# A state-space kernel on one core: the table that orders its 821 operations is written anew

## Chip, cores and metric

The kernel runs on one core of one Trainium2 chip. Times are device microseconds (us) of that core; less is better. The engines are called as the profile calls them: PE (matrix engine; PEld is its weight load), DVE (vector), ACT (scalar), POOL (GpSimd) and SP, which here only issues transfers.

## What is computed

Two sequence operators stand side by side; sequence length is 2048, width 640, everything in bf16. The left half is a diagonal complex state-space layer, the right half a gated long convolution.

```python
# left: A
Lam_bar = exp(exp(log_dt) * (Lambda_re + 1j * Lambda_im))
Bu = einsum("bld,pd->blp", x, ((Lam_bar - 1) / Lam)[:, None] * B)
h[t] = Lam_bar * h[t - 1] + Bu[t]                    # 2048 steps
a = 2 * real(einsum("blp,dp->bld", h, C)) + x * Dskip
# right: B
kv = (sum over t < 4 of shifted(k, t) * shift_k[:, t]) * v
b = q * (causal_convolution(kv, ssm_k) + kv * ssm_D)
out = concatenate([a, b], axis=-1)
```

## The kernel before, in words

Every operation is added to a list by `Program.add` with a name and a number (its place in the list). Most are one instruction; an operation on PE is a group of matmuls into one or two PSUM banks, and its eviction (a copy of the banks to SBUF by ACT or DVE) is an operation of its own. `ORDER` (line 1136) is a string with one entry for each operation: number, engine (A for ACT, V for DVE, G for POOL, T for PE, S for SP) and first bank; a small `t` says that PE does the operation in halves of 64 columns. `Program.emit` (line 123) walks the table and issues each operation on its engine, with waits on those that write or read the same memory or hold the same bank. So the order on each engine is the order of the table, each engine works strictly in that order, and nothing is decided at run time. SP issues nearly all transfers, ACT three at the start.

The left half (`PartA`). `load_B` (line 516) fetches B: blocks 0 and 1 by plain transfers (L524), turned on PE (L531) and evicted by ACT (L533); the rest by two transposing transfers (L519, "the rest of B"). `load_x` (L554) fetches x in eight transposing transfers. `warm` (L546) gives PE ten pairs of matmuls on zeros while it would be idle. `params` (from L357) loads Lambda and log_dt (L369), transposes them by one matmul (L377, "the parameter matmul") and computes powers of Lam_bar on DVE, ACT and POOL, in part by sines (L415, L420, L463). Then the scan in a tree: `up2`, `up1`, `up0` (L588 and L609, evictions L605, L629, L655), a coarse scan on DVE (`coarse`, L673 to L697, with its matmuls at L226 and L230), and `down` (L226, L230, evictions L733, L735). `project` multiplies 16 sets of 128 rows by C (20 matmuls at L226, or 40 at L230), adds x times Dskip (L744) and stores the rows (L780); C comes by L563 and is scaled by L578, evicted at L582. Evictions of `project` are at L768 (ACT, then added at L776) or L770 (DVE).

The right half (`PartB`), in two halves of 320 channels. `load_kv` (L833) fetches k and v of 128 channels by one transposing transfer each, five times (0 to 4); `conv` makes the four taps (L206 or L207, sums L859, product with v L860); `plane` writes the product to DRAM (L866), `relay` reads it back in another layout (L876). `load_h` fetches the filter (L826), a small ssm_D (L813) is added to it at L828. The convolution is a Fourier transform by matmuls: `s1` (L895, in quarters L900; evicted L905), `s2` (L919; L932), a product on DVE or POOL (L943 to L950), back by `r2` (L970; L975) and `r1` (L991; L1007 or L1009, and L1014), times q (L844), stored at L1025.

Some memory is used twice. The half of `VT` that takes the first v is before that scratch for tables: `f1` (DVE, L291) and `i_s` (ACT, L326) read it, and the transfer of the first v waits for both. The groups of `r2` of one half need the whole product of that half (they read what L943 to L950 write).

## Time and profile before

| | |
|---|---|
| median of three runs | 189.14 us (187.04, 189.92, 189.14) |
| the profiled execution | 187.05 us |
| its span, first to last instruction | 185.2 us (1.85 us lie around it) |
| busy PE / PEld / DVE / ACT / POOL | 175.5 / 123.7 / 157.1 / 146.7 / 72.6 us |
| first `up2` group starts, last matmul ends | 9.28 us, 181.8 us |
| granted PE clock | 1.00 |

"L588 PE MATMUL acc<-arena" is a matmul of line 588 that reads the arena (all SBUF memory of the kernel is one tile, `arena`, and all PSUM one, `acc`). In square brackets a row of the timeline gives the idle time before it and what ended it. In the table by stretches each engine has its busy time and the number of its instructions.

### The profile page before, as it was taken

The page shows a single profiled execution, that of the slowest core. Times are in us where ns is not written, and L with a number is a line of the kernel's source. Part 1 is how long each engine was busy: PE and PEld are TensorE (multiplying, and loading weights), DVE is VectorE, ACT ScalarE, POOL GpSimd, SP SyncE. Part 2 cuts the span into 40 slices and gives each one's busy share as a digit, 9 for nine tenths or more (in the row PEclk, how much of TensorE's full clock was granted, in tenths as well). Part 3 has the DMA queues.
Part 4 walks back from the last instruction along what each step waited for, and adds up shares of the span by engine and source line. Part 5 has one row for each costly group of instructions (what it writes and reads, how often), then busy time and mean ns, then how long its engine had stood idle before and what let it go on. Part 6 is the DMA issues. An engine that isn't in the chain of part 4 may idle for free.

```text
span 185.2 us, 7657 instructions
## 1 busy us (share of the span) xinstructions
PE 175.5 (95%) x3399; PEld 123.7 (67%) x3399; DVE 157.1 (85%) x227; ACT 146.7 (79%) x181; POOL 72.6 (39%) x69
## 2 busy tenths in 40 slices
PE   7999999999999999887999999999999999999992
PEld 3554666645768766566686588777578876887771
DVE  3538858699759899998988999999999999898971
ACT  2469697999999998998998998997998883985000
POOL 8669999910000000016704925740730000550630
PEclk9999999999999999999999999999999999999999
DMA  5999999899999989899998479402494993058895
GB/s 156 200 176 141 217 156 130 158 184 192 243 229 225 242 146 164 168 159 164 143 164 225 155 152 128 74 4 85 126 198 107 213 234 86 7 173 200 204 226 159
DMA packets 106827, 30.15 MB, mean 163 GB/s; under 512 B 101291, under 2 KB 106155, under 8 KB 106795
## 3 DMA queue, kind: packets, MB, share of 16 engines
q1 hardware_dynamic: 106476, 29.35, 86.6%
q8 instruction: 26, 0.43, 1.1%
q10 hardware_dynamic: 318, 0.33, 0.5%
q14 instruction: 7, 0.05, 0.1%
HBM read 11.32 MB, written 7.86 MB: 104 GB/s over the span
## 4 chain that ended last, share of the span: by engine, by line
PE 46%; ACT 23%; DVE 14%; SPq 7%; issue 5%; DMA 3%; POOL 0%; ACTq 0%; DVEq 0%; POOLq 0%
PE acc L226 16%; ACT arena L905 8%; PE acc L919 8%; PE acc L230 6%; PE acc L588 5%; DVE arena L735 4%; SPq L554 4%; ACT arena L207 3%; PE acc L970 3%; DMA arena<-in_B_k_dram 3%; ACT arena L932 3%; PE acc L609 3%; PE acc L991 3%; SPq L519 3%; ACT arena L355 2%
## 5 line engine op out<-in xcount | busy, mean ns | idle before, releaser
L588 PE MATMUL acc<-arena 128*64 128x512 bf16 x400 | 45.5, 379 | 0.8 <-DVE arena L420 0.7
L932 ACT CAST arena<-acc 128x960 bf16<-128x960 f32 (+1 forms) x43 | 36.3, 925 | 3.3 <-PE acc L919 2.3
L226 PE MATMUL acc<-arena 128*128 128x320 bf16 (+2 forms) x256 | 36.6, 298 | 1.1 <-ACT arena L905 0.7
L905 ACT CAST arena<-acc 128x1024 bf16<-128x1024 f32 x37 | 36.0, 1027 | 2.1 <-PE acc L900 1.9
L588 PEld LDWEIGHTS <-arena 128*64 128x64 bf16 x400 | 24.3, 110 | 18.4 <-DVE arena L420 1.1
L226 PEld LDWEIGHTS <-arena 128*128 128x128 bf16 x256 | 23.7, 98 | 11.2 <-ACT arena L905 0.8
L860 POOL TENSOR_TENSOR arena<-arena 128x2048 bf16<-128x2048 bf16 x2 | 8.8, 4420 | 51.4 <-DVE arena L859 44.6
L919 PE MATMUL acc<-arena 128*64 128x160 bf16 x512 | 23.3, 235 | 0.6 <-ACT arena L905 0.3
L230 PE MATMUL acc<-arena 128*64 128x320 bf16 (+3 forms) x258 | 23.2, 313 | 0.6 <-DVE arena L697 0.6
L919 PEld LDWEIGHTS <-arena 128*64 128x64 bf16 x512 | 18.5, 110 | 7.2 <-ACT arena L932 1.8
L859 DVE TENSOR_TENSOR arena<-arena 128x2048 bf16<-128x2048 bf16 x14 | 17.8, 1268 | 5.0 <-ACT arena L207 4.7
L735 DVE TENSOR_TENSOR arena<-acc,arena 128x1024 bf16<-128x1024 f32 (+2 forms) x19 | 20.4, 1115 | 0.9 <-PE acc L230 0.6
L776 POOL TENSOR_TENSOR arena<-arena 128x640 bf16<-128x640 f32 x3 | 4.2, 1417 | 32.1 <-ACT arena L768 32.1
L975 ACT CAST arena<-acc 128x1024 bf16<-128x1024 f32 x16 | 15.4, 1025 | 1.6 <-PE acc L970 1.5
L230 PEld LDWEIGHTS <-arena 128*64 128x64 bf16 x258 | 13.0, 110 | 3.6 <-issue 0.7
L895 PE MATMUL acc<-arena 128*64 128x128 bf16 x400 | 14.6, 220 | 0.7 <-ACT arena L605 0.3
L895 PEld LDWEIGHTS <-arena 128*64 128x64 bf16 x400 | 12.6, 110 | 3.6 <-ACT arena L905 0.9
L206 DVE TENSOR_SCALAR arena<-arena 128x2048 bf16<-128x2048 bf16 x15 | 11.0, 748 | 3.6 <-DMA arena<-in_B_k_dram 3.4
L770 DVE TENSOR_TENSOR arena<-acc,arena 128x640 bf16<-128x640 f32 (+1 forms) x14 | 10.8, 772 | 3.3 <-PE acc L226 2.5
L207 ACT ACTIVATE arena<-arena 128x2048 bf16<-128x2048 bf16 (+2 forms) x10 | 11.1, 1111 | 2.9 <-DMA arena<-in_B_k_dram 1.7
L943 DVE TENSOR_TENSOR arena<-arena 128x2560 bf16<-128x2560 bf16 x8 | 11.9, 1483 | 0.1
L609 PE MATMUL acc<-arena 128*64 128x256 bf16 (+2 forms) x140 | 11.5, 291 | 0.2 <-ACT arena L655 0.2
(142 smaller groups left out, 283.2 us busy)
## 6 DMA issues: line engine op xcount, KB each, us to landing
out_dram<-arena SPq DMA_DIRECT2D x31, 160.0 KB, 3.4
arena<-in_B_ssm_k_dram SPq DMA_DIRECT2D x8, 320.0 KB, 5.7
kv_rows<-arena SPq DMA_DIRECT2D x5, 512.0 KB, 3.8
arena<-kv_rows SPq DMA_DIRECT2D x16, 160.0 KB, 3.9
arena<-in_A_x_dram SPq DMA_DIRECT2D x16, 160.0 KB, 3.4
arena<-in_B_q_dram SPq DMA_DIRECT2D x8, 320.0 KB, 5.6
arena<-in_A_B_im_dram ACTq DMA_DIRECT2D x1, 160.0 KB, 2.9
arena<-in_A_B_re_dram SPq DMA_DIRECT2D x1, 160.0 KB, 2.7
```

The source lines that it names most:

```text
L207: self.SM = {nc.scalar: lambda out, in_, by: nc.scalar.mul(out, in_, by), nc.vector: vm(nc.vector), nc.gpsimd: vm(nc.gpsimd)}
L226: e.matmul(out, lhsT=lhsT, rhs=rhs, start=start, stop=stop, skip_group_check=True)
L230: e.matmul(out[half], lhsT=lhsT[:, half], rhs=rhs, start=start, stop=stop, skip_group_check=True, tile_position=(0, 64 * r))
L588: e.matmul(o[64 * r:64 * r + 64], lhsT=self.BT[j][:, r, d, :], rhs=self.XP[:, d, 2 * q:2 * q + 2], start=(d == 0), stop=(d == 4), skip_gro ...
L609: e.matmul(o[64 * r:64 * r + 64], lhsT=self.c.RR[:, n, j, 64 * r:64 * r + 64], rhs=x, start=False, stop=True, skip_group_check=True, tile_ ...
L735: e.tensor_tensor(out=o, in0=b, in1=o, op=ALU.add)
L859: P.add(f"ca{d}_{j}", tt, lambda e: e.tensor_tensor(out=t1, in0=t1, in1=t2, op=ALU.add), outs=[t1], ins=[t1, t2])
L895: e.matmul(B[64 * b:64 * b + 64, 128 * i:128 * i + 128], lhsT=lh[i], rhs=F[:, b, :], start=True, stop=True, tile_position=(0, 64 * b))
L905: P.add(f"e1{what}{hf}_{u}", {PACT: act(1024), PDVE: dve(1024)}, lambda e, B: c.CP[e](out=out, in_=(B.rearrange("p (l n s k) -> p k s l n" ...
L919: e.matmul(B[64 * s:64 * s + 64, 512 * b + 160 * i:512 * b + 160 * i + 160], lhsT=c.W[:, k, 64 * b:64 * b + 64], rhs=self.AS[hf][:, k, 160 ...
L932: c.CP[e](out=out, in_=b.rearrange("p r (k j n) -> p r k j n", k=n, j=4) if nj > 1 else b.rearrange("p r (k x) -> p r k x", k=n))
L975: P.add(f"er2{hf}_{u}", {PACT: act(1024), PDVE: dve(1024)}, lambda e, B: c.CP[e](out=out, in_=B.rearrange("p (s n b) -> p b s n", s=2, n=4 ...
```

## The change

Only the table `ORDER` differs. All 821 operations are still there, and each still waits for what it reads; their order on every engine, the banks, and for some the engine are new. 19 operations went from ACT to DVE, 15 from DVE to ACT, 13 from POOL to DVE and 7 from DVE to POOL; two of the early loads of raw B changed places between SP and ACT. The operations that PE does in halves are 38 where they were 40, not all the same ones. Two lines of it:

```diff
-    "170A0 162G0 163S0 0V0 157G0 6T0 58G0 169A0 164S0 17G0 110G0 19V0 148G0 87V0 11G0 18V0 3T1 89A0 90S0 12G0 42G0 13V0 88S0 "
+    "163A0 12G0 164S0 0V0 87V0 17G0 7T0 67G0 89A0 90S0 18V0 88S0 170A0 8T1 169S0 113G0 22V0 82G0 185S0 6T0 112G0 11G0 9T1 42G0 "
...
```

First place: SP, from the transfers of the rest of B (L519) to the transfer of the second v. L554 is x, L808 shift_k, L833 k or v, L826 the filter, L813 ssm_D. Before:

```order
L519 DMA_TRANSPOSE arena<-in_A_B_im_dram 128x5x384
L808 DMA arena<-in_B_shift_k_dram 128x5x4
L833 DMA_TRANSPOSE arena<-in_B_k_dram 128x2048
L554 DMA_TRANSPOSE arena<-in_A_x_dram 128x5x256
L826 DMA arena<-in_B_ssm_k_dram 32x80x64
L554 DMA_TRANSPOSE arena<-in_A_x_dram 128x5x256
L826 DMA arena<-in_B_ssm_k_dram 32x80x64 x2
L813 DMA arena<-in_B_ssm_D_dram 4x80
L826 DMA arena<-in_B_ssm_k_dram 32x80x64
L833 DMA_TRANSPOSE arena<-in_B_v_dram 128x2048
L833 DMA_TRANSPOSE arena<-in_B_k_dram 128x2048
L554 DMA_TRANSPOSE arena<-in_A_x_dram 128x5x256 x2
```

and now:

```order
L519 DMA_TRANSPOSE arena<-in_A_B_im_dram 128x5x384
L833 DMA_TRANSPOSE arena<-in_B_k_dram 128x2048
L554 DMA_TRANSPOSE arena<-in_A_x_dram 128x5x256
L833 DMA_TRANSPOSE arena<-in_B_k_dram 128x2048
L826 DMA arena<-in_B_ssm_k_dram 32x80x64
L554 DMA_TRANSPOSE arena<-in_A_x_dram 128x5x256
L826 DMA arena<-in_B_ssm_k_dram 32x80x64 x2
L833 DMA_TRANSPOSE arena<-in_B_v_dram 128x2048
L826 DMA arena<-in_B_ssm_k_dram 32x80x64
L813 DMA arena<-in_B_ssm_D_dram 4x80
L554 DMA_TRANSPOSE arena<-in_A_x_dram 128x5x256 x2
```

The second k stands behind the first with one x between them; the first v stands ahead of the last part of the filter and of ssm_D, where it stood behind them; shift_k now goes out earlier, between the x transfers.

Second place: ACT, from the first evictions of `r2` (L975) on; L768 and L1007 are evictions of `project` and `r1`. Before:

```order
L975 CAST arena<-acc 128x256x4 x10
L1007 CAST arena<-acc 128x640 x2
L1007 CAST arena<-acc 128x960
L768 COPY arena<-acc 128x640
L1007 CAST arena<-acc 128x960
L768 COPY arena<-acc 128x640
L1007 CAST arena<-acc 128x960
L975 CAST arena<-acc 128x256x4 x6
L1007 CAST arena<-acc 128x960 x2
```

and now:

```order
L975 CAST arena<-acc 128x256x4 x10
L1007 CAST arena<-acc 128x640 x2
L768 COPY arena<-acc 128x640
L1007 CAST arena<-acc 128x960 x2
L975 CAST arena<-acc 128x256x4 x3
L1007 CAST arena<-acc 128x960
L975 CAST arena<-acc 128x256x4 x5
L1007 CAST arena<-acc 128x640
L1007 CAST arena<-acc 128x960
L768 COPY arena<-acc 128x640
L1007 CAST arena<-acc 128x640
L768 COPY arena<-acc 128x320
```

Of the second ten evictions of `r2` ACT now does eight where it did six (DVE two where it did four), and one of `r1` lies among them. On PE the two last groups of `r1` of the first half, which stood ahead of these ten groups of `r2`, now stand between the fifth and the sixth.

Third place: PE's start. The parameter matmul is L377, L531 turns B, L546 are the warm-up matmuls. Before, up to the first `up2` group: three warm-up pairs, a turn, a pair, two turns, the parameter matmul, three pairs, the fourth turn, three pairs. Now five pairs open, the parameter matmul follows, then all four turns, then five pairs. In the first rows of the difference:

```order
 L546 MATMUL acc<-arena 128x512
+L546 LDWEIGHTS arena
+L546 MATMUL acc<-arena 128x512
+L546 LDWEIGHTS arena
+L546 MATMUL acc<-arena 128x512
+L377 LDWEIGHTS arena
+L377 MATMUL acc<-arena 128x30
 L531 LDWEIGHTS arena
 L531 MATMUL acc<-arena 128x128
```

The plus rows put the parameter matmul ahead of the first turn.

80 rows, old and new, of the table ORDER are left out of this document.

## Prediction

> **What bounds the kernel now.** I read the page's busy shares first, then the busy times by stretches, then the chain that ended last.
>
> ```profile
> PE 175.5 (95%) x3399; PEld 123.7 (67%) x3399; DVE 157.1 (85%) x227; ACT 146.7 (79%) x181; POOL 72.6 (39%) x69
> PE 46%; ACT 23%; DVE 14%; SPq 7%; issue 5%; DMA 3%; POOL 0%; ACTq 0%; DVEq 0%; POOLq 0%
> ```
>
> ```profile
> 9.30:20.00 10.70, 10.01 (x93) 5.28 (x94) 7.12 (x26) 8.38 (x17) 9.14 (x14) 1.00 1.09 175
> 20.00:40.00 20.00, 19.91 (x210) 12.85 (x207) 15.18 (x15) 17.91 (x16) 17.84 (x15) 1.00 1.24 167
> 40.00:60.00 20.00, 19.43 (x310) 12.88 (x306) 16.27 (x24) 19.52 (x28) 0.00 (x0) 1.00 1.12 213
> 60.00:74.00 14.00, 14.00 (x256) 10.05 (x252) 13.06 (x19) 13.13 (x22) 0.00 (x0) 1.00 0.99 181
> 74.00:94.00 20.00, 17.42 (x448) 12.38 (x446) 19.19 (x24) 19.21 (x24) 8.13 (x2) 1.00 1.04 152
> 94.00:110.00 16.00, 15.56 (x398) 11.27 (x396) 14.73 (x16) 15.37 (x18) 7.49 (x3) 1.00 0.83 190
> 110.00:136.00 26.00, 25.54 (x578) 19.24 (x576) 25.01 (x27) 22.74 (x27) 13.15 (x6) 1.00 0.50 91
> 136.00:160.00 24.00, 23.77 (x586) 18.90 (x582) 23.04 (x29) 18.73 (x23) 0.31 (x2) 1.00 0.77 147
> 160.00:166.00 6.00, 6.00 (x166) 5.63 (x165) 5.99 (x7) 5.16 (x6) 4.54 (x3) 1.00 0.34 106
> 166.00:182.00 16.00, 15.78 (x352) 11.44 (x350) 12.86 (x17) 3.22 (x4) 5.01 (x3) 1.00 0.90 217
> ```
>
> Columns: stretch, length, busy PE, PEld, DVE, ACT, POOL, clock, transfers' share, GB/s. PE is nearly always busy; its idle time from 9.3 to 182 us is the sum of the differences: 0.69 + 0.09 + 0.57 + 0 + 2.58 + 0.44 + 0.46 + 0.23 + 0 + 0.22 = 5.3 us. Two engines run beside it at their limit: ACT from 40 to 94 us (19.52 and 19.21 of 20), DVE from 110 to 166. Is a busy PE really working? The pace of a group says so:
>
> ```profile
> 42.22 2.16 PE acc L588 x20
> 67.62 2.16 PE acc L588 x20
> 108.14 2.91 PE acc L230 x40
> ```
>
> The same 20 matmuls at L588 take the same time at both places, so no wait hides inside groups. The kernel is PE's work (which the change leaves alone) plus 9.3 us before it, 5.3 us of gaps and 3.4 us after it. An order can win at most those gaps and part of the start.
>
> [...]
>
> **The change part by part.** Loads per engine hardly move. ACT's 19 leaving operations and 15 arriving ones are nearly all the same kind of evictions (about 1 us each), so both totals stay within some 1 us. Halves instead of whole matmuls cost nothing that the rows show: a `project` takes 2.91 us in 40 halves (L230, above) and 2.89 in 20 whole matmuls (L226, below). So the sum is made from waits.
>
> *Start.*
>
> ```profile
> 0.99 2.74 PE L546 MATMUL acc<-arena 128*128 128x512 bf16 x6 [0.99 <-DVE arena L542]
> 6.28 0.17 PE L377 MATMUL acc<-arena 128*128 128x30 bf16 x1 [0.17 <-DMA arena<-in_A_Lambda_re_dram]
> 6.30 1.47 PE L546 MATMUL acc<-arena 128*128 128x512 bf16 x6
> 7.61 0.44 PE L531 MATMUL acc<-arena 128*128 128x128 bf16 x5
> 9.28 8.82 PE L588 MATMUL acc<-arena 128*64 128x512 bf16 x80
> 18.80 1.05 PE L588 MATMUL acc<-arena 128*64 128x512 bf16 x8 [0.69 <-DVE arena L420]
> 13.18 2.04 POOL L310 TENSOR_TENSOR arena<-arena 128x512 int32<-128x512 int32 x2
> 12.90 0.32 POOL L411 TENSOR_TENSOR arena<-arena 128x80 int32<-128x80 int32 x1
> 14.21 0.27 ACT L415 ACTIVATE arena<-arena 128x80 f32<-128x80 int32 x1
> 14.51 0.81 DVE L420 TENSOR_TENSOR arena<-arena 128x80 bf16<-128x80 f32 x1 [3.42 <-ACT arena L415]
> ```
>
> The parameter matmul waits for a transfer; behind it, from 6.28 to 9.28, PE did six warm-up pairs and a turn, 3.0 us or 0.43 each. Now four turns and five pairs stand behind it, nine times 0.43 = 3.9 us. Its transfers go out one place earlier (0.45 us), so the first `up2` group starts 0.4 to 0.5 us later. Then four groups run, and the fifth met a wait of 0.69: it needs the rest of B and a bank. Both come later now. shift_k (0.59 us of SP) goes ahead of the rest of B. And the bank: on POOL two products of L310 (2.04 us) and one of L351 come ahead of the angles at L411 that the sines at L415 need, some 2.7 us net, of which 0.9 is slack (the angles were ready at 13.2, the sines ran at 14.2); the DVE operations at L420 move from 14.5 to about 16.3, and now both (0.8 + 1.25) stand ahead of the eviction (1.2) that frees the bank: 19.6. The fifth group starts at 19.6 where it started at 18.8: **+0.8** (bounds +0.3, the rest of B alone, and +1.5, sines a further 0.7 late).
>
> *The second k, and 20 to 60 us.*
>
> ```profile
> 14.34 0.59 SPq L808 DMA_DIRECT2D arena<-in_B_shift_k_dram  x1
> 26.43 2.23 SPq L813 DMA_DIRECT2D arena<-in_B_ssm_D_dram  x1
> 28.71 0.43 SPq L826 DMA_DIRECT2D arena<-in_B_ssm_k_dram  x1
> 29.84 4.57 SPq L833 DMA_TRANSPOSE arena<-in_B_v_dram  x1
> 34.45 2.17 SPq L833 DMA_TRANSPOSE arena<-in_B_k_dram  x1
> 20.24 3.22 SPq L554 DMA_TRANSPOSE arena<-in_A_x_dram  x1
> 28.43 1.26 DVE L291 TENSOR_TENSOR arena<-arena 128x256 bf16<-128x256 f32 x1
> arena<-in_B_ssm_k_dram SPq DMA_DIRECT2D x8, 320.0 KB, 5.7
> arena<-in_A_x_dram SPq DMA_TRANSPOSE x8, 5.0
> arena<-in_B_v_dram SPq DMA_TRANSPOSE x5, 6.6
> ```
>
> The transfers' queue is full here (share 1.09 and more), and the same transfers precede the last two x on SP in both orders, so those land no earlier. What the second k delays is the fourth of the eight x that `up1` needs, by its own 2.17 us or, in a fuller queue, some 3: it went out at 20.24 and landed by 20.24 + 5.0 = 25 or 26, now 28 or 29. `up1`, which needs it, stood ninth on PE and stands tenth, at 30.4: covered by one `up2` group of 2.16; without the cover it would cost up to 1 us. The second conv starts with its k at hand, but it stands behind the first on DVE and nothing on PE waits for it at that time: no gain. The first v still waits for `f1` at L291, which ended at 29.7; now it stands behind a sum of taps that waits for ACT's second tap of the first k, and that tap behind a sine and three evictions, to about 28.5; with the sum (1.2) and itself 1.26, `f1` ends at 31. So v goes out at 31.05, not 29.84, and the last filter part and ssm_D, now behind it, land at about 31.05 + 4.57 + 0.43 + 5.7 = 41.8, if the queue is as full as before. DVE waits for them at L828 in order, and PE's first `s1` group at about 42.8: covered by 1 us. The four small gaps from 37 to 59 us, 0.66 together in the rows of 20 to 60, have other groups ahead of them now; I take back **-0.5** (bounds -0.66, all gone, and +1.7, if L828 falls 2.7 us behind).
>
> *74 to 94 us.* Here lie 2.58 of the 5.3 us: PE waits for the coarse scan on DVE and for banks. The new order puts three `s1` groups of k into the scan's shadow, which should remove its 0.7 us; but ACT is full (19.21 of 20) and gets 0.7 us more to evict there. PE's waits cannot fall below what ACT needs. I take **0** (bounds -1.5, half of the gaps, and +1.2).
>
> *The second `r2`.*
>
> ```profile
> 158.85 1.05 PE L991 MATMUL acc<-arena 64*64 64x80 bf16 x96
> 159.84 5.50 PE L970 MATMUL acc<-arena 64*128 64x128 bf16 x160
> 160.59 4.06 ACT L975 CAST arena<-acc 128x1024 bf16<-128x1024 f32 x4
> 165.27 2.89 PE L226 MATMUL acc<-arena 128*128 128x320 bf16 x20
> L975 ACT CAST arena<-acc 128x1024 bf16<-128x1024 f32 x16 | 15.4, 1025 | 1.6 <-PE acc L970 1.5
> ```
>
> PE does two `r1` and ten `r2` groups from 158.9 to 165.3, 6.4 us without a wait, because ACT took six and DVE four evictions. Now ACT has eight of `r2` and one of `r1` in this stretch. `project` 8 follows on the bank whose eviction is ACT's seventh: 0.55 + 7 x 0.9 (ACT starts one every 0.9 when full) = 6.9 us, 0.5 to 0.6 later. Besides, the two `r1` groups covered 1 us in which DVE finished the product; they now stand behind five `r2` groups, so PE meets DVE's end openly, about 0.3. Together **+0.9** (bounds 0, ACT keeping up, and +2.0, evictions at 1.025 apart and the product 0.7 late).
>
> *Sum*, on the profiled execution: 187.05 + 0.8 - 0.5 + 0 + 0.9 = 188.25. That execution was 2.1 us below the median of 189.14; on the median the sum is 190.3. Between the two I forecast **189.3**.
>
> **The rivals.**
>
> *Gaps filled.* If the `s1` groups fill PE's waits from 74 to 94 us and banks come free in time, 2.58 + 0.57 of gaps go and nothing comes back: 189.14 - 3.2 = 186, and up to 1 us less if the start is no later. For it: the coarse scan's waits are DVE latency, not ACT's load. Against: ACT's 19.21 of 20.
>
> *The first v holds up SP.* It is one transfer that waits for a table on DVE, with filter, ssm_D and the last two x behind it. If `f1` is 2 us later than I read (its place follows ACT's second tap), L828 blocks DVE in order, `s1` blocks PE, and convs, relays and `down` all shift: each us beyond the 1 us of cover is lost on PE, and again where DVE evicts late for the `s1` and `up0` groups. At 3.5 us late: 2.5 + 1.5, plus the sum's 1.2 less the 0.5 not regained: 189.14 + 5 = 194. Against: ACT's tap depends on the first k, whose place is unmoved.
>
> *PE falls back to its slow pace.* Its first six warm-up matmuls took 2.74 us, later six 1.47, and the slow pace lasted some 4 us. Now five pairs run and PE waits about 1 us for the parameter transfer. If that wait resets the pace, 4 us at half speed cost 1.9: 191.2. The page's clock column shows 1.00 throughout, so it does not show this. [...]
>
> **How the numbers follow.** Forecast 0.57, gaps filled 0.22, v holds up SP 0.17, slow pace 0.04. A measurement of this kernel can tell about 2% from no change, 185.4 to 192.9. Of gaps filled, whose centre is 186, 0.12 lies beyond 2%, of the v case 0.14; the forecast's own tails give 0.03 and 0.03, the pace 0.01 slow. So faster 0.15, same 0.67, slower 0.18. Half of either outer case is left out: 185.2 to 193.4.
>
> **What would show it.** Right: first `up2` near 9.8, a wait of about 1 us near 19.6, the first v on SP near 31 us, L828 near 41 to 42, about 2.5 us of PE idle between 74 and 94, and waits of PE on ACT at L975 after 159. Wrong: the fourth x ending a wait of PE near 30, L828 after 43, PE idle from 74 to 94 under 1.5 us or over 4, or no wait on ACT in the second `r2`.

## The result, and the profile after

| | before | after |
|---|---|---|
| median (range) | 188.63 us (187.04 to 189.92, 4 runs) | 196.31 us (194.19 to 197.81, 4 runs) |
| profiled execution, its span | 187.05, 185.2 us | 194.19, 192.4 us |

The change makes the kernel slower: ratio 1.041, 95% interval 1.035 to 1.048. The forecast was 189.3 us with a range to 193.4. The comparisons leave disturbed (slower) executions out; the profiles of e3, e7 and e18 are of such executions, and in e18 they were six of twelve, so its ratio and the median of all its executions do not fit together.

The page of the profile after, its busy shares and its clock column (40 slices of the span, tenths of full speed):

```profile
PE 178.9 (93%) x3422; PEld 122.6 (64%) x3423; DVE 163.8 (85%) x235; ACT 146.2 (76%) x177; POOL 73.5 (38%) x67
...
PEclk9999669999999999999999999999999999999998
```

Busy PE rose by 3.4 us although its work is the same but for the operations done in halves, and two slices show 6. Busy time by stretches of the kernel after, columns as in the prediction (length, PE, PEld, DVE, ACT, POOL, clock, transfers' share, GB/s):

```profile
9.30:20.00 10.70, 8.91 (x81) 4.45 (x80) 7.56 (x16) 5.63 (x13) 10.40 (x17) 1.00 1.14 188
20.00:40.00 20.00, 17.10 (x140) 8.37 (x142) 17.32 (x19) 14.39 (x13) 17.83 (x17) 0.83 0.91 124
74.00:94.00 20.00, 17.83 (x434) 12.23 (x432) 19.36 (x26) 18.76 (x25) 5.43 (x2) 1.00 1.03 166
```

From 20 to 40 us PE had 19.91 busy us and 210 matmuls before; now it has 17.10 and 140, and the clock is 0.83. So the loss is early: 1.8 us idle ahead of 20 us, 2.9 behind it, and a slow stretch. From 74 to 94 us it is 17.83 where it was 17.42. The timeline of PE shows the hole:

```profile
9.38 8.82 PE L588 MATMUL acc<-arena 128*64 128x512 bf16 x80
22.90 7.30 PE L588 MATMUL acc<-arena 128*64 128x512 bf16 x46 [4.69 <-DVE arena L605]
```

Four `up2` groups, then 4.69 us of nothing, until DVE has evicted the third group (L605) and its bank is free. The same place took 0.69 us before. The chain that ended last, followed through the hole (start, us, what; two pieces of under 0.05 us are left out):

```profile
15.07 0.28 ACT arena L415
15.38 5.56 DVE arena L420
20.94 0.54 issue
21.48 0.24 DVE arena L420
21.72 1.13 DVE arena L605
22.90 1.49 PE acc L588 x3
```

The sines (L415) are over at 15.35, earlier than the prediction had them. What is long is L420: two DVE operations on 80 elements of each partition, of which the second takes 0.24 us and the first holds DVE from 15.38 to 21.5. The whole two on DVE's timeline, and beside them POOL's:

```profile
15.38 6.34 DVE L420 TENSOR_TENSOR arena<-arena 128x80 bf16<-128x80 f32 x2 [3.03 <-ACT arena L415]
21.63 1.21 DVE L605 CAST arena<-acc 128x1024 bf16<-128x1024 f32 x1
```

```profile
13.64 0.12 POOL L403 IOTA arena<- 64x1 int32 x1
13.73 1.03 POOL L351 TENSOR_TENSOR arena<-arena 128x512 int32<-128x512 int32 x1
14.73 0.31 POOL L411 TENSOR_TENSOR arena<-arena 128x80 int32<-128x80 int32 x1
15.01 1.25 POOL L479 TENSOR_TENSOR arena<-arena 128x640 int32<-128x640 int32 x1
16.22 1.03 POOL L351 TENSOR_TENSOR arena<-arena 128x512 int32<-128x512 int32 x1
17.22 2.03 POOL L310 TENSOR_TENSOR arena<-arena 128x512 int32<-128x512 int32 x2
19.21 1.03 POOL L351 TENSOR_TENSOR arena<-arena 128x512 int32<-128x512 int32 x1
20.21 1.24 POOL L482 TENSOR_TENSOR arena<-arena 128x640 int32<-128x640 int32 x1
21.40 0.22 POOL L809 MEMSET arena<- 128x160 bf16 x1
```

Read the two together: POOL goes from one operation to the next with no idle time, six of them from 15.01 on read memory, and the first L420 ends at 21.57, 0.17 us after POOL has come, at 21.40, to the first one that reads nothing, the MEMSET (an `IOTA` or a `MEMSET` has no operand behind the arrow). This was a reading of one trace; the experiments below test it.

The hole has a price behind it, too. Busy times by stretches of 2 us in the kernel after:

```profile
22.00:24.00 2.00, 1.10 (x6) 0.54 (x8) 2.00 (x3) 2.00 (x3) 2.00 (x4) 0.50 1.08 189
24.00:26.00 2.00, 2.00 (x12) 0.82 (x10) 2.00 (x4) 1.07 (x1) 2.00 (x3) 0.50 1.17 184
26.00:28.00 2.00, 2.00 (x16) 0.92 (x14) 2.00 (x3) 0.00 (x0) 2.00 (x2) 0.68 1.04 100
28.00:30.00 2.00, 2.00 (x22) 0.99 (x18) 2.00 (x4) 0.41 (x1) 2.00 (x3) 1.00 1.24 212
```

The granted clock is 0.50 from 22 to 26 us and 0.68 in the next 2, and the fifth group takes 4.27 us (22.90 to the next one's start at 27.17) instead of 2.16.

### The profile page after: what moved, and what is told of

Same layout as the page of the kernel before. It is cut to its first block, busy times and chain, and to the rows that moved or that the text cites. A ratio compares the mean times of both kernels' runs of the same rounds, so it can differ in the third digit from the quotient of the medians.

```text
span 192.4 us, 7703 instructions
## 1 busy us (share of the span) xinstructions
PE 178.9 (93%) x3422; PEld 122.6 (64%) x3423; DVE 163.8 (85%) x235; ACT 146.2 (76%) x177; POOL 73.5 (38%) x67
## 4 chain that ended last, share of the span: by engine, by line
PE 64%; ACT 12%; DVE 11%; SPq 6%; issue 3%; DMA 2%; DVEq 0%
PE acc L226 19%; PE acc L588 16%; PE acc L230 7%; PE acc L919 5%; SPq L563 4%; DVE arena L735 4%; PE acc L895 3%; PE acc L546 3%; DVE arena L420 3%; ACT arena L932 3%; PE acc L900 3%; ACT arena L975 3%; PE acc L991 2%; DMA arena<-kv_rows 2%; SPq L876 2%
## 5 line engine op out<-in xcount | busy, mean ns | idle before, releaser
L588 PE MATMUL acc<-arena 128*64 128x512 bf16 x400 | 47.3, 393 | 4.7 <-DVE arena L605 4.7
L588 PEld LDWEIGHTS <-arena 128*64 128x64 bf16 x400 | 22.5, 114 | 26.3 <-DVE arena L605 5.2
L226 PE MATMUL acc<-arena 128*128 128x320 bf16 (+3 forms) x263 | 38.6, 299 | 0.5 <-ACT arena L975 0.2
L932 ACT CAST arena<-acc 128x960 bf16<-128x960 f32 (+1 forms) x42 | 35.2, 933 | 4.3 <-PE acc L919 3.4
L905 ACT CAST arena<-acc 128x1024 bf16<-128x1024 f32 x37 | 35.7, 1043 | 1.4 <-PE acc L900 1.1
L226 PEld LDWEIGHTS <-arena 128*128 128x128 bf16 x264 | 24.4, 98 | 10.9 <-ACT arena L975 0.5
L919 PEld LDWEIGHTS <-arena 128*64 128x64 bf16 x512 | 18.7, 110 | 5.9 <-ACT arena L932 2.6
L230 PE MATMUL acc<-arena 128*64 128x320 bf16 (+3 forms) x242 | 21.2, 309 | 0.3 <-DVE arena L655 0.3
L859 DVE TENSOR_TENSOR arena<-arena 128x2048 bf16<-128x2048 bf16 x14 | 17.9, 1281 | 2.1 <-ACT arena L207 1.9
L975 ACT CAST arena<-acc 128x1024 bf16<-128x1024 f32 x18 | 17.0, 1029 | 2.8 <-PE acc L970 2.4
L605 ACT CAST arena<-acc 128x1024 bf16<-128x1024 f32 x8 | 7.9, 1015 | 9.2 <-PE acc L588 9.2
L206 DVE TENSOR_SCALAR arena<-arena 128x2048 bf16<-128x2048 bf16 (+2 forms) x20 | 13.7, 708 | 1.3 <-POOL arena L859 0.7
L946 POOL TENSOR_TENSOR arena<-arena 128x1280 bf16<-128x1280 bf16 x3 | 9.5, 3162 | 12.4 <-DVE arena L943 12.4
L230 PEld LDWEIGHTS <-arena 128*64 128x64 bf16 x242 | 12.1, 110 | 3.1 <-DVE arena L655 0.5
L895 PEld LDWEIGHTS <-arena 128*64 128x64 bf16 x384 | 11.6, 110 | 3.7 <-ACT arena L932 1.1
L1014 POOL TENSOR_TENSOR arena<-arena 128x960 bf16<-128x960 bf16 x2 | 4.5, 2280 | 21.4 <-ACT arena L1007 21.4
L1007 ACT CAST arena<-acc 128x640 bf16<-128x640 f32 (+1 forms) x8 | 6.4, 832 | 7.5 <-PE acc L991 4.6
```

Source lines behind the costliest of these rows:

```text
L206: vm = lambda e: lambda out, in_, by: e.tensor_scalar_mul(out=out, in0=in_, scalar1=by)
L226: e.matmul(out, lhsT=lhsT, rhs=rhs, start=start, stop=stop, skip_group_check=True)
L230: e.matmul(out[half], lhsT=lhsT[:, half], rhs=rhs, start=start, stop=stop, skip_group_check=True, tile_position=(0, 64 * r))
L588: e.matmul(o[64 * r:64 * r + 64], lhsT=self.BT[j][:, r, d, :], rhs=self.XP[:, d, 2 * q:2 * q + 2], start=(d == 0), stop=(d == 4), skip_gro ...
L859: P.add(f"ca{d}_{j}", tt, lambda e: e.tensor_tensor(out=t1, in0=t1, in1=t2, op=ALU.add), outs=[t1], ins=[t1, t2])
L895: e.matmul(B[64 * b:64 * b + 64, 128 * i:128 * i + 128], lhsT=lh[i], rhs=F[:, b, :], start=True, stop=True, tile_position=(0, 64 * b))
```

## The experiments

Starts of the same PE groups, in us, before, after and in the kernels told of below; the same work stands ahead of each in all of them, so a difference that grows or shrinks from row to row says in which stretch time is lost or won:

| PE group | before | after | e2 | e12 | e15 |
|---|---|---|---|---|---|
| first `up2` | 9.28 | 9.38 | 9.46 | 9.23 | 9.33 |
| fifth `up2` on PE | 18.80 | 22.90 | 19.38 | 18.88 | 19.47 |
| the next | 20.95 | 27.17 | 21.53 | 21.03 | 21.63 |
| `project` 0 | 93.82 | 98.84 | 95.15 | 95.31 | 93.23 |
| `project` 11 | 155.80 | 161.44 | 157.79 | 158.11 | 155.88 |
| `project` 8 | 165.27 | 172.06 | 168.55 | 167.35 | 166.65 |

All ratios below are against the order before on the same chip. Of the diffs, the rows are one engine's instructions.

**e1, the changed order once more.** No edit.

> The changed order once more, nothing edited, for a second profile and for what the edited ones are held against. Theory P (the first L420 on DVE reads two operands and gets no turn as long as POOL runs operations that read memory back to back): L420 is long again, 5 to 6 us, the fifth up2 group waits 4 to 5 us and takes about 4.3 us; time 196, ratio 1.04. Theory R (the long L420 was a chance of that one execution): L420 under 1.5 us, the fifth group starts near 19.6, time near 190.

195.37 us, ratio 1.048 (1.042 to 1.054). The first L420 took 6.19 us again (6.19 in the first trace), the wait was 4.63, the fifth group 3.55 us. Theory R falls: it is no chance of one execution.

**e2, the memset early.** On POOL:

```diff
 L411 TENSOR_TENSOR arena<-arena 128x80
 L479 TENSOR_TENSOR arena<-arena 128x640
+L809 MEMSET arena 128x160
 L351 TENSOR_TENSOR arena<-arena 128x512
...
 L482 TENSOR_TENSOR arena<-arena 128x640
-L809 MEMSET arena 128x160
```

> One operation of 0.2 us moves: POOL's memset L809, which reads nothing, from behind L482 to directly behind the second L479 (ends at 16.25). DVE's order, ACT's and PE's are as in the changed order. Theory P: L420 gets its turn at 16.3, its two operations are over by 16.7, the eviction of the third group by 17.9, PE's wait of 4.7 us falls under 0.5, no slow group; all PE starts from the fifth group on are 5.5 to 6.2 us earlier, time 190 to 191, ratio 1.00 to 1.02. Theory D (what costs is that both L420 stand ahead of the eviction on DVE, behind late sines): DVE's order is untouched, so L420 still ends near 21.5 and the time stays 196.

191.91 us, ratio 1.030 (1.023 to 1.037). DVE's timeline, then POOL's:

```profile
15.38 1.15 DVE L420 TENSOR_TENSOR arena<-arena 128x80 bf16<-128x80 f32 x2 [3.03 <-ACT arena L415]
16.43 1.21 DVE L605 CAST arena<-acc 128x1024 bf16<-128x1024 f32 x1
```

```profile
15.01 1.25 POOL L479 TENSOR_TENSOR arena<-arena 128x640 int32<-128x640 int32 x1
16.20 0.22 POOL L809 MEMSET arena<- 128x160 bf16 x1
```

L420 arrives at the same 15.38 and is through at 16.5, as soon as the memset runs. One operation of 0.2 us, moved on another engine, took 5 us off DVE and 5.6 us off the start of the sixth group (27.17 to 21.53). Theory D, that the order on DVE costs it, falls: DVE's order is untouched. The time fell by less than P expected (1.030, not 1.00 to 1.02), since a second wait came up, on L629 at 36.8 us, and the later stretches cost their own; e8 and e12 go after those.

**e3, the eviction first.** On DVE:

```diff
+L605 CAST arena<-acc 128x2x2x256
 L420 TENSOR_TENSOR arena<-arena 128x80 x2
-L605 CAST arena<-acc 128x2x2x256
```

> DVE's eviction of the third up2 group (L605) goes ahead of the two L420; POOL's order is as in the changed order. Theories P and D alike: the bank is free near 16.5, PE does not wait for it at the fifth group, time 190 to 191. Under P L420 is still long and ends near 21.5, or nearly so, only nothing on PE waits for it; under D L420 takes under 1.3 us. If PE waited for the rest of B or for x instead (theory B), the wait stays and the time stays 196.

191.59 us, ratio 1.029 (1.023 to 1.036). No wait for the bank; PE waits 0.89 for the rest of B there. L420, started at 15.39, is 6.35 us long for the two, so it is POOL and not the order on DVE that makes it long, and the eviction behind it that makes it cost.

**e4, PE kept busy in the hole.** On PE, ahead of the fifth `up2` group:

```diff
 L588 MATMUL acc<-arena 64x512
+L546 LDWEIGHTS arena
+L546 MATMUL acc<-arena 128x512
...
 L588 LDWEIGHTS arena
```

> Ten more pairs of warm-up matmuls on zeros, extra work of about 4.3 us, stand on PE directly ahead of the fifth up2 group, where PE waits 4.7 us; nothing else is edited. Theory C (the fifth group took 4.3 us instead of 2.2 because PE's granted clock fell while it waited): the wait for the bank stays, the fifth group takes 2.2 us, the clock column shows 9 throughout, time 196.3 - 2.1 = 194, ratio 1.03. If the slow group has another cause (its operands, transfers), it stays at 4.3 us and the time at 196.

195.88 us, ratio 1.051 (1.043 to 1.059): no gain. But in its place the expectation of C holds, by the timeline of PE:

```profile
18.04 4.30 PE L546 MATMUL acc<-arena 128*128 128x512 bf16 x19 [0.16 <-issue]
22.57 8.61 PE L588 MATMUL acc<-arena 128*64 128x512 bf16 x78 [0.24 <-DVE arena L605]
```

The fifth group starts at 22.57 and the next at 24.76, 2.2 us for a group where the changed order has 4.27, and the granted clock is 1.00 in every stretch from 9.3 to 182 us. So here the idle time caused the slow group. Until `project` 10 this trace is 2.6 us ahead of that of the changed order (154.98 to 157.63); the lead is lost at the end, 2.0 us of it in one wait ahead of an L991 at 176.7 to which the trace puts no cause. The total therefore does not confirm the 2.1 us.

**e5, another pair of operations at the boundary.** On POOL:

```diff
 L411 TENSOR_TENSOR arena<-arena 128x80
+L310 TENSOR_TENSOR arena<-arena 128x512
 L479 TENSOR_TENSOR arena<-arena 128x640
 L351 TENSOR_TENSOR arena<-arena 128x512
-L310 TENSOR_TENSOR arena<-arena 128x512 x2
+L310 TENSOR_TENSOR arena<-arena 128x512
```

> The changed order with one swap on POOL: a product of L310 that reads memory goes ahead of the second L479, so L420 on DVE now arrives during an L310, and the boundary that comes next is L310 to L479, the very pair between which DVE got its turn before the change. The chain of reading operations on POOL is as long as in the changed order and ends near 21.4. Theory P1 (which two operations meet at the boundary decides): L420 takes about 1 us and the run goes as with the early memset, ratio 1.03. Theory P2 (the whole chain of reading operations, however they are paired, keeps DVE out): L420 ends near 21.5 again, 6 us long, ratio 1.045 to 1.05.

194.57 us, ratio 1.037 (1.028 to 1.047); the first L420 6.20 us, the wait 4.8. P2 holds: the pair does not decide.

**e6, the second k alone.** On SP, in the order before:

```diff
-L833 DMA_TRANSPOSE arena<-in_B_k_dram 128x2048
+L833 DMA_TRANSPOSE arena<-in_B_k_dram 128x2048 x2
...
 L833 DMA_TRANSPOSE arena<-in_B_v_dram 128x2048
-L833 DMA_TRANSPOSE arena<-in_B_k_dram 128x2048
```

> The order before, with a single edit: the second load of k stands on SP directly behind the first, ahead of the fourth x, the filter and the first v. What the change is named for, alone. Theory I (it is innocent): the fourth x lands 2 to 3 us later and is covered by up2 groups, the first v goes out 0 to 1 us later; ratio 0.99 to 1.01, no new wait over 0.7 us before 45 us. Theory K (the crowded queue at 20 to 30 us is part of the loss): a wait of PE on an x near 30 us or on L828 near 42 us, 2 to 4 us, ratio 1.01 to 1.02.

188.04 us, ratio 1.000 (0.997 to 1.004). The second k's earlier place, alone, costs nothing that can be measured. It is not free on the way, by PE's timeline:

```profile
29.52 2.35 PE L588 MATMUL acc<-arena 128*64 128x512 bf16 x20 [1.91 <-DMA arena<-in_A_x_dram]
```

PE waits 1.91 us for an x, is 2.1 us late behind it and 1.4 at `project` 0 (95.19), and still the median of ten executions is that of the order before. Theory I said no new wait over 0.7 us and is wrong in that; K's wait came, its price did not.

**e7, before to 60 us, then the changed order.**

```diff
 the first 289 operations of the table before, in their order
+all others in the order of the changed table
```

> The first 289 operations in the order before (to 60.7 us on PE), all others in the changed order. Theory S (the start carries the loss): the first 60 us as before, no wait at the fifth up2 group beyond 0.7 us, and what is left is the rest of the changed order alone: from 64 us to the end it lost 1.9 us in the trace of the changed order and 2.1 with the early memset, so ratio 1.010 (1.005 to 1.015). If the loss lay in the later part, the ratio stays at 1.04.

192.34 us, ratio 1.020 (1.010 to 1.031). Neither expectation. Up to 60 us it runs as before (its starts there are 0.2 us early), but at the joint PE waits 3.4 us for an eviction L655 on DVE, and the group of 20 matmuls behind it takes 4.26 us (63.66 to 67.92) instead of 2.16. The joint makes a wait of its own, so this does not measure the later part. It says only that the loss is not in the later part alone.

**e8, early memset, and the end as before.** Against e2, from 143 us on the order before on all engines; of it, on ACT in the second `r2`:

```diff
-L975 CAST arena<-acc 128x256x4 x3
-L1007 CAST arena<-acc 128x960
-L975 CAST arena<-acc 128x256x4 x5
...
+L975 CAST arena<-acc 128x256x4 x6
+L1007 CAST arena<-acc 128x960 x2
```

> The changed order with the early memset up to its 647th operation (143 us), then the rest in the order before, so that DVE again takes four of the ten evictions of the second r2 and the two last r1 groups of the first half stand ahead of it. Theory E (ACT's eight evictions cost 0.9 to 1.5 us there, the step of the prediction): no wait of PE on ACT at L975 after 159 us, ratio 1.022 against the 1.030 of the early memset alone. If the stretch costs nothing that the evictions' engine explains, the ratio stays 1.03.

191.25 us, ratio 1.019 (1.009 to 1.029). The ten groups again run without a hole:

```profile
163.52 5.52 PE L970 MATMUL acc<-arena 64*128 64x128 bf16 x160
168.97 2.89 PE L226 MATMUL acc<-arena 128*128 128x320 bf16 x20
```

From `project` 11 to `project` 8 it takes 9.24 us, as before (9.47), where the changed order takes 10.62 and e2 10.76: 1.5 us back. The two ratios' intervals overlap, so the total is only consistent with it. That ACT's evictions cost this, as E has it, is not shown: the edit puts back more than ACT's order, and in e2 PE's rows show no wait on ACT at that place. Where the time lay is told with the second `r2` below.

**e9, the two L420 apart.** On DVE, in the changed order:

```diff
-L420 TENSOR_TENSOR arena<-arena 128x80 x2
+L420 TENSOR_TENSOR arena<-arena 128x80
 L605 CAST arena<-acc 128x2x2x256
+L420 TENSOR_TENSOR arena<-arena 128x80
```

> The changed order with one edit on DVE: the second L420 goes behind the eviction of the third up2 group, as it stood before the change. POOL's order is the changed one. Theory P2 (POOL's chain of reading operations keeps any two-operand L420 out until it ends near 21.4): the first L420 is 6 us long as in the changed order, the bank comes no earlier, ratio 1.04 to 1.05. Theory Q (two such operations in a row on DVE are what loses the turn): the first L420 gets its turn at 16.3, the eviction ends near 17.5, no wait over 1.1 us at the fifth group, ratio 1.02 to 1.03.

196.24 us, ratio 1.041 (1.030 to 1.052); L420 6.19 us, wait 4.5. P2 holds, Q falls.

**e10, the two L420 in a row, in the order before.** On DVE:

```diff
-L420 TENSOR_TENSOR arena<-arena 128x80
+L420 TENSOR_TENSOR arena<-arena 128x80 x2
 L605 CAST arena<-acc 128x2x2x256 x2
-L420 TENSOR_TENSOR arena<-arena 128x80
```

> The order before with one edit on DVE: the second L420 goes directly behind the first, ahead of both evictions of up2 that stood between them. This is the move on which the prediction's start rests, alone. Theory of the prediction (late sines plus two short operations ahead of the eviction): the first L420 gets its turn at 15.2 as before, the second is over by 16.4 at the latest, the evictions run 0.2 to 1.0 us later, PE waits at most 0.5 us more, ratio 0.995 to 1.005. Theory Q (two in a row lose the turn): both stand until POOL's next operation that reads nothing, the L306 at 18.6; evictions end at 20 and 21.2, the fifth group starts 1.5 to 2.5 us later, ratio 1.01.

188.13 us, ratio 0.997 (0.992 to 1.002). Both L420 are over in 1.77 us, started at 14.76. The move on which the prediction's start rested is worth nothing, as the prediction's own working has it, when DVE gets its turns.

**e11, the loads as before.** On SP, against e8:

```diff
-L808 DMA arena<-in_B_shift_k_dram 128x5x4
...
 L519 DMA_TRANSPOSE arena<-in_A_B_im_dram 128x5x384
+L808 DMA arena<-in_B_shift_k_dram 128x5x4
 L833 DMA_TRANSPOSE arena<-in_B_k_dram 128x2048
...
-L833 DMA_TRANSPOSE arena<-in_B_k_dram 128x2048
```

> The order with the early memset and with the order before from 143 us on, and on SP the first 21 loads as before the change too: the rest of B ahead of shift_k, the second k behind the first v. Theory L (what is left of the loss is the crowded queue): the waits on x (0.9), on B (0.6) and the late evictions at L629 (1.4) fall to under 1 us together, ratio 1.00 to 1.01 where that order without this edit had 1.019. Theory M (what is left is DVE, whose operations with two operands still stand behind POOL's): the wait on L629 stays at 1.4 or grows, ratio 1.015 to 1.02.

194.71 us, ratio 1.031 (1.021 to 1.041), where e8 had 1.019 (1.009 to 1.029): no gain, and a new wait that neither theory had. In the changed order ACT takes L814, which reads shift_k, ahead of the sines. By ACT's timeline:

```profile
19.00 0.21 ACT L814 CAST arena<-arena 128x20 f32<-128x20 bf16 x1 [6.25 <-DMA arena<-in_B_shift_k_dram]
```

With shift_k late, ACT stands 6.25 us, the sines end at 21.1, and PE's wait is 5.3. The question about the queue stays open here; but the case shows that the early shift_k is a part of the new order that cannot be undone alone.

**e12, the second L463 later.** On DVE, against e8:

```diff
-L463 TENSOR_TENSOR arena<-arena 128x640 x2
+L463 TENSOR_TENSOR arena<-arena 128x640
...
 L629 CAST arena<-acc 128x2x2x256
+L463 TENSOR_TENSOR arena<-arena 128x640
```

> The order with the early memset and with the order before from 143 us on, and one more edit on DVE: the second L463 of 28 to 32 us, which takes 1.66 us beside POOL and 0.81 alone, goes behind the eviction L629 that PE waits for at 36 us. Theory W (the second wait, too, is DVE's two-operand operations standing behind POOL's): the eviction starts 1.2 to 1.7 us earlier and PE's wait on L629 of 1.4 to 1.7 us falls under 0.5; all later starts 1 us earlier if nothing else is late there, ratio 1.010 to 1.016 where it was 1.019. If the eviction waits for PE or a transfer instead, the wait stays.

189.66 us, ratio 1.011 (1.003 to 1.019). DVE's timeline in e12:

```profile
28.34 1.66 DVE L463 TENSOR_TENSOR arena<-arena 128x640 int32<-128x640 int32 x1
29.93 2.06 DVE L859 TENSOR_TENSOR arena<-arena 128x2048 bf16<-128x2048 bf16 x1
...
33.09 1.02 DVE L441 TENSOR_TENSOR arena<-arena 128x20 f32<-128x20 f32 x1
34.02 1.21 DVE L629 CAST arena<-acc 128x1024 bf16<-128x1024 f32 x1
```

PE's wait on L629 falls from 1.4 to 0.29 us; another of 1.0, on L605, appears at 39 us. W holds for the first, but `project` 0 starts only 0.2 us earlier than in e8 (95.31 for 95.47). Three DVE operations with two operands are some 0.85 us longer there than the shortest of the same shape in other traces (L463 1.66 for 0.82 in before, L859 2.06 for 1.21 and L441 1.02 for the 0.17 of an L443 in e2). That one of them, moved, made the eviction earlier is shown; that the others delay it in the same way is argued.

**e13 and e14, POOL's order inside the chain.** On POOL, e13 in the order before, e14 in the changed one:

```diff
 L411 TENSOR_TENSOR arena<-arena 128x80
-L310 TENSOR_TENSOR arena<-arena 128x512 x2
 L479 TENSOR_TENSOR arena<-arena 128x640
-L310 TENSOR_TENSOR arena<-arena 128x512
+L310 TENSOR_TENSOR arena<-arena 128x512 x3
```

```diff
 L411 TENSOR_TENSOR arena<-arena 128x80
+L310 TENSOR_TENSOR arena<-arena 128x512 x2
 L479 TENSOR_TENSOR arena<-arena 128x640
 L351 TENSOR_TENSOR arena<-arena 128x512
-L310 TENSOR_TENSOR arena<-arena 128x512 x2
+L482 TENSOR_TENSOR arena<-arena 128x640
```

> The order before with one edit on POOL: the second L479 goes directly behind the angles L411, ahead of two products of L310, as L479 stands behind L411 in the changed order. The first L420 then arrives at 14.5 with a chain of five reading operations before POOL's next L306. If the place of L479 right behind the angles is what shuts DVE out until the chain ends, the first L420 is 4.2 us long (to 18.7), the two evictions end at 20 and 21, and the loss of the start shows in the order before: fifth group 2 to 3 us later, ratio 1.01 to 1.02. If not, L420 gets its turn at the next boundary (15.4) and the ratio is 0.995 to 1.005.

> The changed order with POOL's operations behind the angles L411 put as nearly as possible as they stood before: L310, L310, L479, then an L351 and the L482 that reads what that L479 wrote, then an L351 and an L482, then the memset. The chain is one operation longer and would end near 22.5. If that pattern is what let DVE in before the change, the first L420 gets its turn at 16.1 or 17.1 and the run is as with the early memset, ratio 1.03. If it does not, L420 is 7 us long, the wait at the fifth group is near 5.8 us, ratio 1.045 to 1.055.

e13: 187.08 us, ratio 0.999 (0.995 to 1.002), L420 0.97 us. e14: 195.75 us, ratio 1.042 (1.034 to 1.050), the two L420 7.55 us, PE's wait 6.03. The order inside the chain does not decide either. In e14 the chain ends 1.2 us later (22.66 for 21.45) and the wait is 1.3 longer, which is P2 once more.

**e15, the small iota away from the chain.** On POOL, in the changed order:

```diff
-L403 IOTA arena 64x1
+L403 IOTA arena 64x1 x2
...
 L409 TENSOR_TENSOR arena<-arena 128x10
-L403 IOTA arena 64x1
 L351 TENSOR_TENSOR arena<-arena 128x512
 L411 TENSOR_TENSOR arena<-arena 128x80
```

> The changed order with one edit on POOL: the last of the four small iotas L403, which write 64 of the 128 partitions and of which the changed order has one at 13.6 us directly ahead of the chain, goes behind another L403 at 11.9. The chain of reading operations from 13.7 to 21.4 and DVE's order stay. Theory H (an operation on half of the partitions leaves POOL's two halves out of step, so that in a chain of reading operations there is never a moment at which both have let go): the first L420 gets its turn at the next boundary, 16.3, the run is as with the early memset, ratio 1.03. If not, L420 is 6 us long and the ratio 1.04 to 1.05.

189.47 us, ratio 1.012 (1.004 to 1.020). DVE's timeline, and then POOL's:

```profile
15.36 1.99 DVE L420 TENSOR_TENSOR arena<-arena 128x80 bf16<-128x80 f32 x2 [2.94 <-ACT arena L415]
17.27 1.21 DVE L605 CAST arena<-acc 128x1024 bf16<-128x1024 f32 x1
```

```profile
15.00 1.25 POOL L479 TENSOR_TENSOR arena<-arena 128x640 int32<-128x640 int32 x1
16.21 1.03 POOL L351 TENSOR_TENSOR arena<-arena 128x512 int32<-128x512 int32 x1
17.21 2.03 POOL L310 TENSOR_TENSOR arena<-arena 128x512 int32<-128x512 int32 x2
```

Everything from 13.7 to 21.4 us is as in the changed order to 0.02 us: POOL's chain, its times, DVE's arrival. Only an IOTA of 0.12 us on 64 of the 128 partitions is no longer ahead of it. And the two L420 are over at 17.35, behind the first two boundaries that POOL comes to (16.21 and 17.21), where the changed order has them over at 21.72. (The moment of L420's arrival does not explain it: it comes 0.36 us behind the start of that L479, and 0.37 us behind it in the changed order and in e1.) The ratio is better than the 1.03 that H expected. By the timeline of PE, what the fifth group waits for is now a transfer:

```profile
19.47 11.85 PE L588 MATMUL acc<-arena 128*64 128x512 bf16 x108 [1.32 <-DMA arena<-in_A_B_im_dram]
```

**e16 and e17, the small iota put ahead of the chain in the order before.** On POOL, e16 and e17:

```diff
-L403 IOTA arena 64x1
 L409 TENSOR_TENSOR arena<-arena 128x10 x3
 L479 TENSOR_TENSOR arena<-arena 128x640
+L403 IOTA arena 64x1
 L411 TENSOR_TENSOR arena<-arena 128x80
```

```diff
-L403 IOTA arena 64x1
 L409 TENSOR_TENSOR arena<-arena 128x10 x3
+L403 IOTA arena 64x1
 L479 TENSOR_TENSOR arena<-arena 128x640
```

> The order before with one edit on POOL: one of the small iotas L403 (64 partitions) goes from 10.8 us to directly ahead of the angles L411, so that it precedes the chain of reading operations as in the changed order. Theory H: the first L420 is shut out until POOL's L306 at 18.7, 4.1 us instead of 0.8; the evictions end at 20 and 21, the fifth group starts 2 to 3 us later, ratio 1.01 to 1.02. If not, L420 takes 0.8 us and the ratio is 0.995 to 1.005.

> The order before with one edit on POOL: a small iota L403 (64 partitions) goes between the last L409 and the first L479, so that the chain of L479, the angles and five more reading operations follows it directly; in the run with the late L403 POOL stood still for 0.08 us behind it, in the changed order it does not. Theory H2 (an L403 on 64 partitions and no pause behind it shuts DVE out for the chain): the first L420 stands until POOL's L306 near 18.8, over 4 us long; the evictions end at 20 and 21, the fifth group starts 2 to 3 us later, ratio 1.01 to 1.02. If not, L420 takes 0.3 to 1.0 us and the ratio is 0.995 to 1.005.

e16: 187.85 us, ratio 1.001 (0.997 to 1.006), L420 0.25 us. e17: 187.46 us, ratio 1.003 (0.999 to 1.007), L420 about 1.0 us. The wait did not come, so in the order before H fails as e16 states it. In both POOL pauses behind the L403; e16:

```profile
12.81 0.13 POOL L403 IOTA arena<- 64x1 int32 x1
13.02 0.32 POOL L411 TENSOR_TENSOR arena<-arena 128x80 int32<-128x80 int32 x1
```

12.94 to 13.02 is idle; in e17 it is 11.73 to 11.81. In the changed order the L351 behind the L403 starts at 13.73, before that one's end at 13.76. The condition that H2 names, no pause, was thus not made, and was not tried in the order before.

**e18, the terms together.** Against e15, on SP and on ACT, and behind 143 us the order before:

```diff
-L808 DMA arena<-in_B_shift_k_dram 128x5x4
...
 L519 DMA_TRANSPOSE arena<-in_A_B_im_dram 128x5x384
+L808 DMA arena<-in_B_shift_k_dram 128x5x4
```

```diff
-L814 CAST arena<-arena 128x20
...
 L605 CAST arena<-acc 128x2x2x256
+L814 CAST arena<-arena 128x20
```

> What the runs point to, put together: the changed order with the early L403, from 143 us on the order before, and at the start the rest of B ahead of shift_k on SP, with ACT's L814 that reads shift_k behind the eviction of the fourth up2 group instead of ahead of the sines. By the terms of the traces: the early L403 alone ended 1.4 us above the order before; the end as before takes 1.4 off, the rest of B another 0.5. Forecast ratio 0.997 (0.990 to 1.004): level with the order before, not clearly faster.

Ratio 0.998 (0.994 to 1.002); the median of all twelve executions is 188.71 us against 187.46. The two L420 take 1.98 us again, so a second trace shows what taking the IOTA away does. The terms add up to the order before and no further. With the parts that cost it undone, the new order is level; no version here is faster than the kernel before.

## Why the prediction was wrong

**What bounds the kernel: right in the main.** PE's work is the same but for half a microsecond (the second `r2`, below), and the time went into PE's waits and into its clock.

**The start: the step that failed.** It put the fifth group at +0.8 us (bounds +0.3 to +1.5), because "both (0.8 + 1.25) stand ahead of the eviction (1.2) that frees the bank: 19.6". It came at +4.1, and the group behind it at +6.2. The steps ahead of that one were harmless: the first `up2` came 0.1 us later, not 0.4 to 0.5, and the sines a little early. What was wrong is what 0.8 and 1.25 are. They were read as L420's work, and they were mostly waits for POOL: alone it takes 0.24 us, and in the trace of before each of its two rows ends 0.1 us after an operation of POOL that reads: the first at 15.32, the two L310 at 15.22, and the second so, by DVE's timeline and POOL's:

```profile
17.50 1.25 DVE L420 TENSOR_TENSOR arena<-arena 128x80 bf16<-128x80 f32 x1
```

```profile
17.39 1.25 POOL L482 TENSOR_TENSOR arena<-arena 128x640 int32<-128x640 int32 x1
```

The one ends at 18.75, the other at 18.64. So what bounds these times here is POOL's chain, not L420's own work. The chain in the new order ends at 21.45; with 0.24 for the second L420 and 1.2 for the eviction, the bound was 22.9 us and not 20.3, and that is where the group started. e15 closes the sum: with DVE getting its turns, in the same order otherwise, the fifth group starts at 19.47, +0.7. That this is near the +0.8 is luck: the bank is free at 18.48 there, and PE waits for the rest of B, which the prediction had at +0.3. The step took its durations from a trace in which POOL lets DVE in, as if there were no other case.

**The slow pace: the right rival in the wrong place.** It had a chance of 0.04, which was the author's estimate, was laid at the parameter matmul and priced at 1.9 us. No run shows that cost there: in the trace of after PE comes to the parameter matmul at 5.23 us without a wait, and the ten warm-up matmuls behind it take 2.34 us, where six took 1.47 before. Nor did it happen behind the 0.69 us wait in the trace of before, where the group took 2.15 us (18.80 to 20.95). Behind the hole it did happen, at a cost of 2.1 us in the trace (4.27 less 2.16). e4, which fills the hole, removes it. Once a wait is bounded at 4 us rather than 1.5, this rival belongs to the same bound. The runs show a slow pace behind waits of 4.5 to 6.0 us in six traces (after, e1, e5, e9, e11, e14, with a mean granted clock of 0.979 to 0.991 over the execution where the kernel before has 1.00) and behind one of 3.4 us in e7, and none behind waits of 1.7 to 2.0 us in three (e2 and e6, where the groups behind them took 2.19 and 2.16 us, and e4, where the 40 matmuls of `project` behind it took 5.61 us as in after). In e3 the clock fell to 0.50 behind a wait of 2.11 us, and a `project` of 20 matmuls took 4.56 us instead of 2.89, by the timeline of PE:

```profile
100.92 0.70 PE L900 MATMUL acc<-arena 64*64 64x64 bf16 x64 [2.11 <-DVE arena L828]
101.55 4.56 PE L226 MATMUL acc<-arena 128*128 128x320 bf16 x20
```

So where above 2 us a wait becomes dear is not settled here.

**The second k, 20 to 60 us, and 74 to 94 us: inside the bounds, wrong on the way.** The text gave 0.5 us back up to 60 us (at most 0.66) and nothing from 74 to 94. From the sixth group to `project` 0 it was 1.2 together (6.2 to 5.0); from the last `up2` group to `project` 0 (67.46 to 93.82 us before, 73.28 to 98.85 after) PE is idle for 2.17 us where it was 2.58, so 0.4 of it lies there. Without the hole the same stretch gave 1.3 back in e15 (+0.7 to -0.6) and lost 0.8 in e2 (+0.6 to +1.3), where PE waited 1.7 us for L629 on DVE. The tables of the two differ on POOL alone, so the size of this term hangs on more than the gaps it was read from. The fourth x was covered in the changed order, but not with the second k alone (e6: 1.9 us, where the text gave up to 1 us for the case without cover). The first v went out at 37.09 us, not 31, and L828 ran at 44.5, not 41 to 42; in e15, without the hole, they are at 32.3 and 39.9. PE did not wait for L828 in either, so the rival in which the first v holds up SP, though its 194 us comes near the result, is not what happened.

**The second `r2`: near in size, wrong in cause.** +0.9 was forecast (0 to 2.0); `project` 11 to 8 takes 10.62 us instead of 9.47, +1.15, and e8 gives it back. The timeline of PE in the kernel after shows where:

```profile
167.93 1.17 PE L967 MATMUL acc<-arena 64*64 64x128 bf16 x32
169.03 0.95 PE L970 MATMUL acc<-arena 64*128 64x128 bf16 x23
170.37 1.51 PE L970 MATMUL acc<-arena 64*128 64x128 bf16 x41 [0.39 <-issue]
172.06 2.89 PE L226 MATMUL acc<-arena 128*128 128x320 bf16 x20 [0.18 <-ACT arena L975]
```

About half of it is work and not a wait: one of the ten groups, which PE did whole before, is now done in halves (L967, 32 matmuls for 16). It takes 1.10 us to the start of the next, where a group takes 0.54 (ten in 5.43 us before). The prediction held that halves cost nothing, from the two rows of `project`, where it is so; it did not look at `r2`. Another 0.39 us is a stall without a named cause, and only 0.18 us is the forecast wait on ACT. In e2 and e15, with the same order on ACT, the stall is 0.60 us and the row of the L226 behind these groups shows no wait on ACT. The 0.3 us for the end of the product did not come. That the number is near is luck.

Of the stall the traces show one thing more. In after, e2 and e15 it stands ahead of the 24th of these 64 matmuls, 0.39 to 0.60 us long; e1, e3, e5, e9 and e14 have one of 0.4 to 1.1 us ahead of an L970 too. In e4, which puts 20 more matmuls ahead of them, it stands ahead of the 4th, 0.73 us long, and the stall of 2.0 us at 176.7 us follows 256 recorded matmuls later. So from after to e4 it stayed at the same count of PE's matmuls, of which 20 were new, and not at the same matmul. Its cause is not shown.

**The sum, with the measured start.** By the table: +6.2 at the sixth group, -1.2 to `project` 0, +0.6 to `project` 11, +1.2 to `project` 8: 6.8 us, of the 7.1 between the two profiled executions. The +0.6 between `project` 0 and 11 was in no step.

**What stays open.** Shown: in the changed order the first L420 stands behind POOL's chain until an operation that reads nothing (e2 against e1, e5, e9, e14), and taking one IOTA on 64 partitions away from the chain's head ends that (e15, e18). Not shown: why that IOTA does it. Theory H was the author's guess about what happens inside POOL, and no trace shows the inside of POOL. Its two forecasts for the order before failed (e16, e17), so the IOTA is not enough by itself; a pause of 0.08 us behind it may be the difference, which no run tests.

## What to carry to other kernels

A duration in a trace is not a cost: before reusing a short DVE operation's time elsewhere, look for what else ends when it ends, and bound it by that engine's whole unbroken chain (here to 21.45 us). When an order is written anew, look at what stands on POOL beside DVE operations with two operands such as L420, and try an operation that reads nothing inside a long chain of POOL's reads (here a memset: the two L420 took 1.15 us in e2 instead of 6.34). An iota was no safe choice for it here: with one on 64 partitions ahead of the chain the two took 6.34 us, without it 1.99 (e15). A wait bounded at several us had a second price here, PE's clock: 1.4 to 2.1 us behind waits of 4.5 to 6.0 us. It belongs in the same bound. And a number that comes out right may have another cause: split the measured stretch into work and waits before calling a step right.

## What the runs showed of the hardware that was not expected

- One DVE operation on 80 elements of each partition took 0.24, 0.8, 1.25 or 6.19 us, by what POOL did beside it. It was shut out through five boundaries between POOL operations that read in the trace of after, in e1, e3, e4, e5 and e9, and through six in e14. In e2, with the memset at 16.20, both L420 were over at 16.53. In the changed order POOL's next boundary behind the arrival of L420 was at 16.22, and the first L420 ended at 21.57: there the wait lasted for a chain.
- 0.12 us of work on half the partitions, at 13.64 us on POOL, decided over about 4.4 us of DVE's time (the two L420 take 6.34 us in the trace of after and 1.99 in e15).
- An `r2` group done in halves took 1.10 us where a whole one took 0.54; for `project` the two forms took 2.91 and 2.89 us.
- A hole of 4.5 to 6.0 us on PE cost 1.4 to 2.1 us more in the group behind it (3.5 to 4.3 us instead of 2.16).
